# Blocked loads of q and k with VectorE transposes in place of TensorE transposes, for the last two batch pairs of a retention and FFN kernel

## The chip, the cores and the metric

The kernel runs on one core of a Trainium2 chip. The metric is the device time of one execution in microseconds. Three executions of the kernel before took 886.32, 886.95 and 888.02 us; the median is 886.95 us. A further execution was recorded by the hardware profiler, and every figure of the profile is from that one.

## The reference

Two blocks follow each other, all in float32 (weights arrive as float64):

```python
# retention: q, k, v are (8, 8, 576, 64) = batch, heads, sequence, head_dim
scores = matmul(q, k.T) / sqrt(64)
gamma  = 1 - 2 ** (-5 - arange(8))            # one per head
Dmat   = where(i >= j, gamma ** (i - j), 0)   # i, j: positions
attn   = matmul(scores * Dmat, v)
# bridge: (B, H, S, D) -> (B*S, H*D) = (4608, 512)
a = x @ w1; b = x @ w2                        # d_model 512, d_ff 1024
out = ((a * b) @ w3) @ w_out
```

The kernel writes the decay as a product: q is multiplied by gamma^i / sqrt(64) and v by gamma^-j, with a triangular mask in each chunk and a running state over the chunks before it. Both decay tables are inputs of the launch (`decay_q` of 8 x 576, `decay_k` of 576 x 8).

## The kernel before

**Chunks.** Batches are taken in four pairs. The sequence of 576 is cut into NC = 5 chunks, the first of 64 tokens and four of 128. A chunk g (0 to 19) is chunk g mod 5 of pair g div 5; it holds 2 batches x 8 heads. Chunks 5, 10 and 15 are the short ones.

**One chunk.** `load` (line 100) brings q, k and v with tokens in the 128 partitions, each as one DMA of 256 B runs (one head's 64 floats). `scale` (162) multiplies q or v by its decay on GpSimd. `front` (174) turns k and q: for each batch and pair of heads one TensorE transpose (line 185) of tokens x 128 features, 8 for k and 8 for q, into four PSUM tiles, which ScalarE copies to `kT` and `qT` (188). `score` (191) multiplies them (200) and VectorE masks the result into `pm` (203). `state` (207) adds k^T v of the chunk to a running PSUM tile (221), except in the last chunk of a pair, and copies it (225); it reads k with tokens in the partitions. `pv` (228) forms the output: state times qT (249, not in a pair's first chunk) and pm times v (256).

**FFN.** `up` computes one quarter of the hidden width for 2 x 192 tokens as seven TensorE products (451); VectorE sums them (456) and multiplies the two halves (477) as its last operation. Before the first quarter of a token block `strassen_tokens` (425) forms sums of the tokens, on GpSimd in the part of interest. `down` multiplies 2 x 128 tokens by the merged last weights (557), with VectorE sums (561), and issues its stores (602) on SP's queue. `carry` (509) is one ScalarE copy.

**Order.** The schedule is written by hand: each engine runs its instructions in the order in which the code emits them. SP's queue, too, issues DMAs in emitted order and waits for a buffer before a load. The first pair (chunks 0 to 4) runs among the conversion of weights. Then a loop over steps g = 5 to 19 emits, in each step, the load of q and k of chunk g+2, the scaling of v and the `front` of chunk g+1, about half of the step's work items, `pv(g)`, the load of v of g+2, `state` and `score` of g+1, the scaling of q of g+2, and the rest of the work items. A work item is an `up`, a `down` or a `carry`; they come from a list that a finished pair refills. From step 10 on a step has three or four of them, before that one. The two that stand ahead of `pv` are, for instance, two `up` in steps 10, 12, 14 and 17, an `up` and then a `down` in 11, 15 and 18, a `down` and then an `up` in 13, an `up` and a `carry` in 16.

**Buffers.** The tiles of loaded q, k and v have two buffers each, `kT` one in this loop, `qT` two, `pm` one, the output tile of `down` one. PSUM has seven rotating accumulation tiles (`acc`) and one for the state.

Of the kernel before, what the change touches and what calls it, by code (L numbers as in the profile page):

```python
# [8 lines left out]
F32 = mybir.dt.float32  # L9
I32 = mybir.dt.int32  # L10
U32 = mybir.dt.uint32
ALU = mybir.AluOpType
PSUM = bass.MemoryType.PSUM

# [19 lines left out]
def kernel(  # L36
# [13 lines left out]
    nc = tc.nc  # L50
    moe_w1, moe_w2, moe_w3, moe_w_out = (
        w.bitcast(I32).rearrange("r (c t) -> r c t", t=2) for w in (moe_w1, moe_w2, moe_w3, moe_w_out))
    B, H, S, D = q.shape
# [3 lines left out]
    P = 128  # L57
    NP = H // 2
# [3 lines left out]
    NC = (S + P - 1) // P  # L62
    short = S - (NC - 1) * P
    sizes = [short] + [P] * (NC - 1)
    starts = [0] + [short + c * P for c in range(NC - 1)]
    G = NB2 * NC
# [9 lines left out]
    const = ctx.enter_context(tc.tile_pool(name="const", bufs=1))  # L76
# [8 lines left out]
    pools = {}  # L85

    def open_attention(part):
        for nm in ("ld", "fr"):
            pools[nm] = part.enter_context(
                tc.tile_pool(name=nm, bufs=2, side="right", reuse_waits="tile"))  # L90

    open_attention(att_part)
    acc = ctx.enter_context(tc.tile_pool(name="acc", bufs=7, space=PSUM))
    st_ps = ctx.enter_context(tc.tile_pool(name="st_ps", bufs=1, space=PSUM))

    ctx.enter_context(tc.manual_schedule())

    live = {}

    def load(g, names, engine=nc.sync):  # L100
        i, c = divmod(g, NC)
        sz = sizes[c]
        src = {"k": k, "q": q, "v": v}
        for nm in names:
            t = pools["ld"].tile([P, 2 * H, D], F32, tag="ld_" + nm, name="ld_" + nm)
            engine.dma_start(
                t[:sz], src[nm][2 * i:2 * i + 2, :, starts[c]:starts[c] + sz, :].rearrange("b h p d -> p (b h) d"))
            live[nm, g] = t
# [13 lines left out]
    nc.vector.memset(lim[:, 1:2], 255.0 * 2.0 ** 23)  # L122
    gk = const.tile([P, NC, H], F32, tag="gk", name="gk")
    gq = const.tile([P, NC, H], F32, tag="gq", name="gq")
    dq = ffn.tile([P, 4, 2, TB], F32, tag="c", name="dq", bufs=1).rearrange("p a b s -> p (a b s)")[:H, :S]
    nc.scalar.dma_start(dq, decay_q)
    nc.scalar.dma_start(gk[:short, 0, :], decay_k[:short, :])
# [4 lines left out]
    for c in (0, slice(1, NC)):  # L132
        n = short if c == 0 else P
# [8 lines left out]
    def A(fp, nm):  # L142

        h, m = divmod(fp, 2)
        if nm in ("S1", "S2", "S4"):
            return wS[h][:, ("S1", "S2", "S4").index(nm), m]
        r, f = {"A11": (0, 0), "A12": (1, 0), "A21": (0, 1), "S3": (0, 1), "A22": (1, 1)}[nm]
        return wA[h][:, :, 2 * r:2 * r + 2, m * QC + f * P:m * QC + f * P + P]

    def strassen_weights(fp):  # L150
        def tt(out, in0, in1, op):
            nc.vector.tensor_tensor(out=A(fp, out), in0=A(fp, in0), in1=A(fp, in1), op=op)

        tt("S1", "A21", "A22", ALU.add)
        tt("S2", "S1", "A11", ALU.subtract)
        yield
        tt("S3", "A11", "A21", ALU.subtract)
        tt("S4", "A12", "S2", ALU.subtract)
        live["S", fp] = True
        yield  # L160

    def scale(g, nm, scalar=False):
        c = g % NC
        sz = sizes[c]
        t, gam = live[nm, g], {"q": gq, "v": gk}[nm]
        t = t[:sz].rearrange("p (b h) d -> p b h d", b=2)
        if scalar:
            for h in range(H):
                nc.scalar.mul(t[:, :, h, :], t[:, :, h, :], gam[:sz, c, h:h + 1])
            return  # L170
        nc.gpsimd.tensor_tensor(  # L171
            out=t, in0=t, in1=gam[:sz, c].unsqueeze(1).unsqueeze(3).to_broadcast([sz, 2, H, D]), op=ALU.mult)

    def front(g, names="kq"):
        c = g % NC
        sz = sizes[c]
        for nm in names:
            src = live[nm, g]
            dst = pools["fr"].tile([P, 2, NP, P], F32, tag=nm + "T", name=nm + "T",
                                   bufs=1 if nm == "k" and g >= NC else 2)  # L180
            for b in range(2):
                tp = acc.tile([P, NP, P], F32, tag="acc", name="tp")
                for p in range(NP):
                    h = b * H + 2 * p
                    nc.tensor.transpose(tp[:, p, :sz],  # L185
                                        src[:sz, h:h + 2, :].rearrange("p a d -> p (a d)"),
                                        ident[:sz, :sz])
                nc.scalar.copy(dst[:, b, :, :sz], tp[:, :, :sz])
            live[nm + "T", g] = dst

    def score(g):
        c = g % NC
        sz = sizes[c]
        kT, qT = live["kT", g], live["qT", g]
        pm = pools["fr"].tile([P, 2, 2, NP, P], F32, tag="pm", name="pm", bufs=1)
        for b in range(2):
            sc = [acc.tile([P, NP, P], F32, tag="acc", name="sc") for j in range(2)]
            for p in range(NP):
                for j, hs in enumerate(heads):
                    nc.tensor.matmul(sc[j][:sz, p, :sz], kT[hs, b, p, :sz], qT[hs, b, p, :sz],  # L200
                                     start=True, stop=True)
            for j in range(2):
                nc.vector.tensor_mul(pm[:sz, b, j, :, :sz], sc[j][:sz, :, :sz],  # L203
                                     mask[:sz, :sz].unsqueeze(1).to_broadcast([sz, NP, sz]))
        live["pm", g] = pm

    def state(g):
        c = g % NC
        sz = sizes[c]
        if c == NC - 1:  # L210
            return
        kn, vs = live["k", g], live["v", g]
        if c == 0:
            live["st"] = st_ps.tile([P, 2, NP, D], F32, tag="st", name="st")
        st = live["st"]

        for b in range(2):
            for p in range(NP):
                for j, hs in enumerate(heads):
                    h = b * H + 2 * p + j  # L220
                    nc.tensor.matmul(st[hs, b, p, :], kn[:sz, h, :], vs[:sz, h, :],  # L221
                                     start=(c == 0 and b == 0 and p == 0), stop=(c == NC - 2),
                                     skip_group_check=True)
        sb = pools["fr"].tile([P, 2, NP, D], F32, tag="sb", name="sb")
        nc.scalar.copy(sb, st)
        live["sb", g + 1] = sb
# [309 lines left out]
    def ahead(x, y, n=3):  # L536
        todo_sums = pair_of(x, y)[2]
        for _ in range(min(n, len(todo_sums))):
            aside.append(todo_sums.pop(0))
# [75 lines left out]
    score(0)  # L615
    scale(0, "v")
    state(0)
    convert_up_to(1)
    pv(0)
# [8 lines left out]
    scale(1, "v")  # L628
    score(1)
    state(1)  # L630
    convert_up_to(3)
    load_block()
    convert_up_to(4)
    first_sums = strassen_weights(0)
    next(first_sums)
    pv(1)
# [12 lines left out]
    convert(2)  # L649
    score(2)  # L650
    state(2)
    scale(3, "v", True)
    front(3, "q")
# [18 lines left out]
    att_part.close()  # L672


    pools["ab3"] = weights_part.enter_context(tc.tile_pool(name="ab3", bufs=1, side="right", reuse_waits="tile"))
    pools["wst"] = w3_part.enter_context(tc.tile_pool(name="wst", bufs=2, side="right", reuse_waits="tile"))
    w3op = ctx.enter_context(tc.tile_pool(name="w3op", bufs=1, reuse_waits="tile"))
# [60 lines left out]
    def work(n):  # L738
        for _ in range(min(n, len(todo))):
            fn, *args = todo.pop(0)  # L740

            nxt = next((x for x in todo if x[0] is not carry), None)
            if nxt and nxt[0] is down and fn is not carry:
                if fn is down:
                    args.append(nxt[1:])
                else:
                    last = args == [*every[max(nxt[1][0], nxt[2][0])], NQ - 1]
                    ahead(*nxt[1:], 1 if last else 3)
            fn(*args)
# [4 lines left out]
    state(NC)  # L754
    score(NC)
    scale(NC + 1, "q")
    for g in range(NC, G):
        c = g % NC
        n = -(-len(todo) // (NC - c))
        if g + 2 < G:  # L760
            load(g + 2, "kq")
        if g + 1 < G:
            scale(g + 1, "v")
            front(g + 1)
        work((n + 1) // 2)
        pv(g)
        if g + 2 < G:
            load(g + 2, "v")
        if g + 1 < G:
            state(g + 1)  # L770
            score(g + 1)
        if g + 2 < G:
            scale(g + 2, "q")
        if g == NC + 1:
            strassen_tokens(1, 0)
            todo.extend((up, 1, 0, fp) for fp in range(2))
        work(n // 2)
        if c == NC - 1:
            add_pair(g // NC)
# [44 lines left out]
```

## Time and profile before

| | |
|---|---|
| median of three executions | 886.95 us (886.32 to 888.02) |
| the profiled execution | 887.59 us, its span 885.9 us, mean TensorE clock 0.998 |
| TensorE busy (PE) | 866.6 us, 98% |
| VectorE / ScalarE / GpSimd busy | 433.7 / 212.4 / 111.1 us |
| all PE transposes of q and k | 320, of which 160 belong to chunks 10 to 19 |
| GpSimd scaling of q (line 171) | 18 of 1.9 us |
| DMA moved | 59.73 MB, 110,592 of the packets being 256 B runs of q, k and v |

The span is what the profiler saw from the first to the last instruction; the execution's own time is a little more. In the profile PE is TensorE's matmul, PEld its weight load, DVE VectorE, ACT ScalarE, POOL GpSimd and SPq the queue of SP. L185 is line 185 of the kernel. A row of a timeline gives the start in us from the span's start, the time in us, engine, line, operation, `output<-input`, and in brackets how long the engine was idle before it and what ended that. The chain is followed back from the last instruction through whatever released each step; rows of it give start, time and what ran.

### The profile page before, as it was taken

Reading aid. Unit: us, or ns where it says so; the run is one execution under the profiler, and the core shown is the slowest. Engines: PE = TensorE matmul, PEld = TensorE weight load, DVE = VectorE, ACT = ScalarE, POOL = GpSimd, SP = SyncE. Lnnn points to the kernel's source line nnn. Section 1 sums busy time; section 2 is a strip of 40 time slices with the busy share of each in tenths; the row PEclk is TensorE's granted clock in tenths of the full one; section 3 lists DMA queues with packets and bytes.
Section 4 is the critical chain, followed back from the end, with each engine's and each line's share of the span. In section 5 each row is a group of like instructions: output and inputs, shape, how many; then the busy total and the mean of one; then the engine's idle time right before and its main releaser. Section 6 shows DMA issues by size and latency. Waiting matters only on the chain.

```text
span 885.9 us, 15255 instructions
## 1 busy us (share of the span) xinstructions
PE 866.6 (98%) x6517; PEld 792.8 (89%) x6517; DVE 433.7 (49%) x763; ACT 212.4 (24%) x426; POOL 111.1 (13%) x82
## 2 busy tenths in 40 slices
PE   5899999999999999999999999999999999999998
PEld 4799999544889999999999999999999999999997
DVE  3799998971543243433434433433433424434343
ACT  3676334552122212111121111211110111001000
POOL 3000020003003223002112121221200101000000
PEclk9999999999999999999999999999999999999999
DMA  9993332427046533134033134022100000000001
GB/s 184 217 229 99 96 118 97 143 95 107 0 108 124 105 60 73 26 72 96 1 72 61 25 72 95 1 57 40 26 24 24 1 24 1 24 24 1 24 1 47
DMA packets 125555, 59.73 MB, mean 67 GB/s; under 512 B 113704, under 2 KB 113704, under 8 KB 125488
## 3 DMA queue, kind: packets, MB, share of 16 engines
q1 hardware_dynamic: 123824, 58.47, 29.9%
q8 instruction: 51, 0.84, 0.4%
q10 hardware_dynamic: 1664, 0.30, 0.2%
q14 instruction: 16, 0.13, 0.1%
HBM read 49.32 MB, written 9.44 MB: 66 GB/s over the span
## 4 chain that ended last, share of the span: by engine, by line
PE 89%; DVE 3%; issue 1%; DMA 1%; ACT 1%; ACTq 0%; SPq 0%; DVEq 0%
PE up L451 45%; PE po L557 24%; PE ps L406 6%; PE xps L256 4%; PE sc L200 3%; PE tp L185 3%; PE xps L249 2%; PE st L221 1%; DVE c L456 1%; PE tp L396 1%; DVE e L341 0%; DMA raw<-in_moe_w_dram 0%; ACT e L330 0%; DVE w L350 0%; DVE ab L477 0%
## 5 line engine op out<-in xcount | busy, mean ns | idle before, releaser
L456 DVE TENSOR_TENSOR c<-up,c 128x384 f32<-128x384 f32 x240 | 133.6, 557 | 224.3 <-PE up L451 218.0
L451 PE MATMUL up<-xT,wA 128*128 128x192 f32 x1152 | 212.6, 328 | 0.9 <-ACT xT L261 0.9
L451 PEld LDWEIGHTS up<-xT,wA 128*128 128x128 f32 x1152 | 191.0, 191 | 3.2 <-ACT xT L261 1.1
L451 PE MATMUL up<-T,wS 128*128 128x192 f32 x768 | 141.7, 328 | 2.1 <-DVE T L425 2.1
L451 PEld LDWEIGHTS up<-T,wS 128*128 128x128 f32 x768 | 128.3, 191 | 2.4 <-issue 2.4
L557 PE MATMUL po<-w3o,ab 128*128 128x256 f32 x456 | 104.1, 380 | 0.3 <-ACT ot L579 0.3
L557 PEld LDWEIGHTS po<-w3o,ab 128*128 128x128 f32 x456 | 85.9, 190 | 12.2 <-ACT ot L579 0.7
L471 ACT COPY c<-up 128x384 f32<-128x384 f32 x48 | 22.9, 477 | 228.1 <-PE up L451 223.9
L561 DVE TENSOR_TENSOR ot<-po,ot 128x256 f32<-128x256 f32 x90 | 38.2, 424 | 74.8 <-PE po L557 74.2
L451 PE MATMUL up<-xT,wS 128*128 128x192 f32 x384 | 70.6, 327 | 0.6 <-DVE c L456 0.5
L451 PE MATMUL up<-T,wA 128*128 128x192 f32 x384 | 70.3, 326 | 0.0
L203 DVE TENSOR_TENSOR pm<-sc,mask 128x512 f32<-128x512 f32 (+1 forms) x80 | 45.5, 629 | 48.0 <-PE sc L200 48.0
L557 PE MATMUL po<-wB,forms 128*128 128x256 f32 x288 | 65.1, 379 | 0.0
L451 PEld LDWEIGHTS up<-xT,wS 128*128 128x128 f32 x384 | 63.6, 190 | 1.5 <-DVE c L456 1.5
L451 PEld LDWEIGHTS up<-T,wA 128*128 128x128 f32 x384 | 63.7, 190 | 0.0
L557 PEld LDWEIGHTS po<-wB,forms 128*128 128x128 f32 x288 | 54.7, 190 | 7.4
L171 POOL TENSOR_TENSOR ld_q<-ld_q,gq 128x1024 f32<-128x1024 f32 (+1 forms) x18 | 34.8, 1931 | 209.7 <-DMA ld_q<-in_q_dram 204.4
L406 PE MATMUL ps<-wo,w3T 128*128 128x512 f32 x128 | 56.4, 593 | 0.2 <-ACT w3T L398 0.2
L171 POOL TENSOR_TENSOR ld_v<-ld_v,gk 128x1024 f32<-128x1024 f32 (+1 forms) x17 | 32.3, 1900 | 176.5 <-DMA ld_v<-in_v_dram 144.1
L425 POOL TENSOR_TENSOR T<-xT,T 128x384 f32<-128x384 f32 x20 | 21.2, 1058 | 228.9 <-PE up L451 227.2
L477 DVE TENSOR_TENSOR ab<-c 128x768 f32<-128x768 f32 x48 | 46.4, 967 | 3.8
L406 PEld LDWEIGHTS ps<-wo,w3T 128*128 128x128 f32 x128 | 23.7, 190 | 27.3 <-issue 26.8
(72 smaller groups left out, 829.1 us busy)
## 6 DMA issues: line engine op xcount, KB each, us to landing
raw<-in_moe_w_dram SPq DMA_DIRECT2D x24, 512.0 KB, 3.8
ld_k<-in_k_dram SPq DMA_DIRECT2D x16, 512.0 KB, 6.5
ld_q<-in_q_dram SPq DMA_DIRECT2D x16, 512.0 KB, 7.1
ld_v<-in_v_dram SPq DMA_DIRECT2D x16, 512.0 KB, 4.7
out_dram<-ot SPq DMA_DIRECT2D x24, 256.0 KB, 2.1
raw<-in_moe_w_dram SPq DMA_DIRECT2D x16, 256.0 KB, 6.4
raw<-in_moe_w_out_dram SPq DMA_DIRECT2D x8, 512.0 KB, 3.5
out_dram<-ot SPq DMA_DIRECT2D x24, 128.0 KB, 2.4
```

The source lines that it names most:

```text
L171: nc.gpsimd.tensor_tensor(out=t, in0=t, in1=gam[:sz, c].unsqueeze(1).unsqueeze(3).to_broadcast([sz, 2, H, D]), op=ALU.mult)
L185: nc.tensor.transpose(tp[:, p, :sz], src[:sz, h:h + 2, :].rearrange("p a d -> p (a d)"), ident[:sz, :sz])
L200: nc.tensor.matmul(sc[j][:sz, p, :sz], kT[hs, b, p, :sz], qT[hs, b, p, :sz], start=True, stop=True)
L203: nc.vector.tensor_mul(pm[:sz, b, j, :, :sz], sc[j][:sz, :, :sz], mask[:sz, :sz].unsqueeze(1).to_broadcast([sz, NP, sz]))
L256: nc.tensor.matmul(banks[r][heads[half], b, n, :sz], vs[:sz, b * H + 2 * p + j, :], pm[:sz, b, j, p, :sz], start=(c == 0 and m == 0), stop ...
L406: nc.tensor.matmul(ps, live["w3T", ft][:, g, :], live["wo"][:, g, :], start=(g == 0), stop=(g == KF - 1))
L451: nc.tensor.matmul(ps[:, w, :], a[:, w, r, :], b[:, r, :], start=(new and w == r == 0), stop=(w == r == 1), skip_group_check=True)
L456: nc.vector.tensor_add(c[:, to], ps, c[:, sb])
L471: nc.scalar.copy(c[:, 0], p1)
L477: nc.vector.tensor_mul(ab[:, 4 * fp:4 * fp + 4, :], c[:, :, 0, :], c[:, :, 1, :])
L557: nc.tensor.matmul(ps[nm], a[A][:, f, :], live["W"][B][:, f, :], start=(f == 0 and not on), stop=(f == NP - 1), skip_group_check=True)
L561: nc.vector.tensor_add(ot[:, to[0], to[1]], ps[nm], ot[:, sb[0], sb[1]])
```

## The change

For chunks 10 to 19 the TensorE transposes are replaced. q and k are loaded a second way, `load_blocks`: each 32 tokens x 32 features block of a head goes to the partitions where its features will stand once transposed, with the 32 tokens in those 32 partitions and the features along the free dimension. A chunk of 128 tokens needs 4 feature groups x 4 token groups = 16 DMAs for q and 16 for k, each of 32 partitions, 8 segments and 128 B runs; a chunk of 64 tokens needs half as many. Then one VectorE transpose (32x32 blocks) for k and one for q writes the whole of `kT` and `qT`. The scaling of q, two GpSimd operations of 512 elements per partition, is done on the blocks, with decays in a new constant tile `gqs`, filled by 16 small DMAs with 4 B runs. k is still loaded the plain way, too, for `state`, except in the last chunk of a pair. The blocked tiles use the two buffers of the plain q tile.

In the loop, for such chunks: the loads of k and blocks of g+2 are emitted after `pv(g)` and the load of v, not at the step's start; the scaling of q of g+1 comes after the first work item, and the transposes of g+1 after the second, directly ahead of `pv(g)`. In step 9, which has one work item, both come after it. The sequence of the work items is as before.

```diff
+    gqs = const.tile([P, NP, S // 32], F32, tag="gqs", name="gqs")
...
+    BL = 32
+    def load_blocks(g, nm):
+        i, c = divmod(g, NC)
+        n = sizes[c] // BL
+        t = pools["ld"].tile([P, 2 * NP, P // BL, BL], F32, tag="ld_q", name="bl_" + nm)
+        src = {"k": k, "q": q}[nm][2 * i:2 * i + 2].rearrange("b (p a) s d -> a (b p) s d", a=2)
+        for a in range(2):
+            for f in range(D // BL):
+                part = (a * (D // BL) + f) * BL
+                for m in range(n):
+                    s0 = starts[c] + m * BL
+                    nc.sync.dma_start(t[part:part + BL, :, m, :],
+                                      src[a, :, s0:s0 + BL, f * BL:(f + 1) * BL].rearrange("m r x -> r m x"))
+        live["bl_" + nm, g] = t
+    def scale_blocks(g):
...
+        for b in range(2):
+            part = t[:, b * NP:(b + 1) * NP, :n, :]
+            nc.gpsimd.tensor_tensor(
+                out=part, in0=part, in1=gqs[:, :, n0:n0 + n].unsqueeze(3).to_broadcast([P, NP, n, BL]),
+                op=ALU.mult)
+    def front_blocks(g):
...
+        for nm in "kq":
+            dst = pools["fr"].tile([P, 2, NP, P], F32, tag=nm + "T", name=nm + "T", bufs=1 if nm == "k" else 2)
+            nc.vector.transpose(
+                dst[:, :, :, :sizes[c]].rearrange("p b m (n x) -> p (b m) n x", x=BL),
+                live["bl_" + nm, g][:, :, :n, :])
+            live[nm + "T", g] = dst
...
     att_part.close()
+    for a in range(2):
+        for f in range(D // BL):
+            part = (a * (D // BL) + f) * BL
+            for p in range(NP):
+                nc.sync.dma_start(gqs[part:part + BL, p, :], decay_q[2 * p + a].rearrange("(n r) -> r n", r=BL))
...
+    in_blocks = [u >= 2 * NC for u in range(G)] + [False] * 2
     for g in range(NC, G):
         c = g % NC
         n = -(-len(todo) // (NC - c))
-        if g + 2 < G:
+        if g + 2 < G and not in_blocks[g + 2]:
             load(g + 2, "kq")
         if g + 1 < G:
             scale(g + 1, "v")
-            front(g + 1)
-        work((n + 1) // 2)
+            if not in_blocks[g + 1]:
+                front(g + 1)
+        half = (n + 1) // 2
+        if in_blocks[g + 1]:
+            work(1)
+            scale_blocks(g + 1)
+            work(1)
+            front_blocks(g + 1)
+            half = max(half - 2, 0)
+        work(half)
         pv(g)
         if g + 2 < G:
             load(g + 2, "v")
+        if in_blocks[g + 2]:
+            if (g + 2) % NC != NC - 1:
+                load(g + 2, "k")
+            load_blocks(g + 2, "k")
+            load_blocks(g + 2, "q")
         if g + 1 < G:
             state(g + 1)
             score(g + 1)
-        if g + 2 < G:
+        if g + 2 < G and not in_blocks[g + 2]:
             scale(g + 2, "q")
```

More of the change, by code (lines that the diff above doesn't have):

```diff
@@ L160, in strassen_weights @@
         yield
+    BL = 32
[13 more added lines that the diff above has]
+    def scale_blocks(g):
+        c = g % NC
+        n, n0 = sizes[c] // BL, starts[c] // BL
+        t = live["bl_q", g]
+        for b in range(2):
[4 more added lines that the diff above has]
+    def front_blocks(g):
+        c = g % NC
+        n = sizes[c] // BL
+        for nm in "kq":
[4 more added lines that the diff above has]
+            live[nm + "T", g] = dst
     def scale(g, nm, scalar=False):
@@ L211, in state @@
             return
-        kn, vs = live["k", g], live["v", g]
+        vs = live["v", g]
+        kn = live["k", g]
         if c == 0:
```

## The prediction

> **What bounds the kernel now.** I read the page's busy times first, then the chain that ended last, then VectorE and the DMA queue's issues around one step.
>
> The page, busy time and chain by engine:
>
> ```profile
> PE 866.6 (98%) x6517; PEld 792.8 (89%) x6517; DVE 433.7 (49%) x763; ACT 212.4 (24%) x426; POOL 111.1 (13%) x82
> PE 89%; DVE 3%; issue 1%; DMA 1%; ACT 1%; ACTq 0%; SPq 0%; DVEq 0%
> ```
>
> TensorE is the bound. Whatever leaves it shortens the run, and whatever makes it wait lengthens it. The chain in order of time (start, us, what), three stretches; a step g is named by its pv:
>
> ```profile
> 331.52 1.03 PE xps L249 x32
> 332.55 1.90 PE xps L256 x32
> 334.45 1.02 PE st L221 x30
> ...
> 336.45 1.90 PE tp L185 x16
> ...
> 356.56 1.08 PE xps L256 x32
> 357.63 1.08 PE st L221 x32
> 358.72 1.99 PE sc L200 x32
> ...
> 567.25 9.10 PE up L451 x56
> 576.35 1.03 PE xps L249 x32
> 577.38 1.90 PE xps L256 x32
> 579.28 0.93 PE st L221 x32
> 580.21 1.99 PE sc L200 x32
> ```
>
> The first is pv of step 9 with the PE transposes of chunk 11 behind it, the second pv of step 10 (a first chunk of 64 tokens, so no L249), the third step 16. From a pv's start to the score behind it PE has 3.86 us of other work in step 16 and only 2.16 us in step 10. VectorE there (timeline, same columns):
>
> ```profile
> 576.38 0.56 DVE L456 TENSOR_TENSOR c<-up,c 128x384 f32<-128x384 f32 x1 [2.04 <-PE up L451]
> 577.05 0.96 DVE L477 TENSOR_TENSOR ab<-c 128x768 f32<-128x768 f32 x1
> ```
>
> After an `up`, VectorE is done 1.66 us into pv (578.01 - 576.35); after a `down` 0.46 us into it (last L561, 405.06 + 0.42 against 405.02). The issues on SP's queue and on ACT's, from their timelines:
>
> ```profile
> 473.54 2.25 SPq L106 DMA_DIRECT2D ld_q<-in_q_dram  x1
> 505.82 0.37 SPq L106 DMA_DIRECT2D ld_v<-in_v_dram  x1
> 64.89 1.25 SPq L291 DMA_DIRECT2D raw<-in_moe_w_dram  x2
> 1.58 0.79 ACTq L126 DMA_DIRECT2D dq<-decay_q_dram  x1
> ```
>
> An issue over 128 partitions takes 0.37 us with a free queue; two over 64 partitions take 1.25 us, 0.65 us apart with the gap; one over 8 partitions 0.79 us. A full load right behind another takes 2.0 to 2.3 us[...].
>
> [...] The trace has no VectorE transpose. Its two-source rows (384 elements 557 ns, 768 elements 967 ns) give 1.07 ns per element and 0.15 us fixed. [...] Here 256 B runs move at 221 to 240 GB/s in 410 to 416 us, 18.6 ns per run on each of 16 engines. [...]
>
> **What is removed.** The 16 PE transposes of each of chunks 10 to 19, from the chain: 0.98, 1.90, 1.75, 1.75, 1.90, 1.14, 1.75, 1.75, 1.75, 1.75 = **16.4 us**, all on the path. With them go four ACT copies of 0.6 us a chunk (ACT is 24% busy) and two accumulation tiles; both were hidden and are worth nothing. POOL's scaling of q (1.90 us) goes too.
>
> **What is added.** (1) *gqs*: 16 DMAs behind the raw loads of the early weight phase. At 0.65 us that is 10.4 us of SP. The raw load issued at 116.0 goes into the buffer freed by the block five before it, and its own block is read first near 136; 16 us are left after a 4 us landing, so it costs nothing. Its 9,216 runs of 4 B take at most 10.7 us of the 16 engines at 18.6 ns each, under the same cover. If that cover were gone, the one delay of 10 us would count. (2) *Block loads*: 32 issues a step (16 for 64-token chunks) behind v and, except for last chunks, k. In runs, 8192 of 128 B: 4.8 us at half of 18.6 ns, 9.5 us at the full value; either is under the issue time. The old q load, and k at the step's start, go. (3) *Scalings*: two POOL operations of 512 elements, 1.2 us each between the rows of 384 (1.06) and 1024 (1.90): 2.4 us. (4) *Two VectorE transposes* of 1024 elements. [...] 1.25 us each, 2.6 us with hand-overs, near 1.4 for a short chunk.
>
> **VectorE's order.** The transposes stand behind the second work item's sums and ahead of the mask products of the score; they end 1.66 + 2.6 = 4.26 us into pv after an `up`, 3.06 after a `down`. The score of chunk g+1 needs both. Stall against the start of that score in the trace: steps 9 and 14 (short chunk next) none; 10: 4.26 - 2.16 = 2.1; 11: none; 12, 16, 17: 0.4 each; 13: 4.26 - 2.93 = 1.3; 15: 3.06 - 2.16 = 0.9; 18: 0.1. Sum 5.6 us. Behind the waiting transposes nothing but those mask products queues.
>
> **SP's order.** v waits for the end of pv(g), as before; then k, then the blocks. For a full chunk: pv 2.9, v 0.5, k 2.1[...] = 5.5 us after pv's start; 32 issues; 2.0 us landing of the last (the stores' row: 2.0 to 3.5); 2.4 us scaling; 1.3 us transposing q. What does an issue over 32 partitions cost? Between 0.40 with gap (the 128-partition row) and 0.85 (the 8-partition row); I take the 64-partition pair, 0.65. Then q is ready 5.5 + 20.8 + 2.0 + 2.4 + 1.3 = 32.0 us after pv's start. Time to the score that needs it, PE transposes taken out:
>
> - loaded in step 9, used in 10: 358.72 - 331.52 - 1.90 = 25.3 us: stall 6.7, in place of the 2.1;
> - loaded in 8, used in 9 (16 issues): ready 4.7 + 10.4 + 2.0 + 1.3 + 0.8 = 19.2 against 335.47 - 316.32 - 0.98 = 18.2: stall 1.0;
> - loaded in 12 without k: 3.5 + 26.5 = 30.0 against 30.0: within VectorE's 1.3;
> - loaded in 10, 11, 14, 15, 16, 17: 50, 37, 41, 35, 49 and 51 us: covered.
>
> Stores of a `down` behind block loads start up to some 10 us late; each next `down` comes at least an `up` (9.1 us) later, so output tiles stay covered. Waits of the added operations on many loads: an estimate of 0.15 us a step, 1 us, from the 17 to 51 ns of the wait instructions shown.
>
> **Sum.** Loss 5.6 - 2.1 + 6.7 + 1.0 + 1.0 = 12.2; gain 16.4; net 4.2 us faster. The profiled execution took 887.59 us (span 885.9, 1.7 around it), so 883.4 there; against the median 886.95, 0.6 above which the profiled one lies, **882.7**.
>
> **Rivals.**
> - *Almost all the gain arrives.* At 0.45 us an issue[...], steps 9 and 10 aren't late for loads: loss 5.6 + 1 = 6.6, time 877[...]. For: 128-partition issues take 0.37. Against: everything narrower took 0.5 to 0.8.
> - *SP's issues become the bound (slower).* Place: 32 small issues between a pv and the score of the next step. Each 0.01 us more costs 0.16 us in step 9, 0.32 in step 10 and, past 0.69, 0.32 in step 13. Loss equals gain at 0.72 us an issue; at 0.85 it is 4.2 + 13.1 + 1.2 + 6.4 + 2.9 in steps 9, 10, 12, 13, 16, 1.4 in the others, 1.0 waits: 30, so 900. For: issue time grew from 128 to 64 partitions. Against: the 0.79 is a first issue on another queue.
> - *Transposes at half rate (slower).* They take 4.6 us a pair and end 6.3 us into pv, 5.1 after a `down`: 4.2 to 1.2 us in each full step, 7.9 in step 10 with its loads: 27.7 in all, time 898. It turns slower when a pair takes about 3.1 us. [...]
> - *No effect*: only if the freed PE time were already idle. The chain has PE on it throughout, so this is small beyond a chance meeting of gain and loss.
>
> **Chances.** Forecast and near it (878 to 887) 0.43; most of the gain (below 878) 0.17; SP as bound 0.23; slow transposes 0.15; no effect 0.02. This kernel's measurement can tell about 0.2%, 1.8 us. Of the first case a fifth lies within that: faster 0.52, same 0.10, slower 0.38. The likeliest case's own range is 878 to 887. Eight in ten reaches from part of the better case to both slow ones: 874 to 900.
>
> **What would show it.** No PE transposes after 336 us; two VectorE transposes a chunk of about 1.25 us; 32 issues about 0.65 us apart on SP after each pv; a PE wait ahead of the score of about 7 us in step 10, 1 to 2 in steps 13 and 15, none in step 11. If transposes take 2 us, or issues 0.8, the sign turns. A PE wait inside the early weight phase would mean that gqs was not covered.

## The result and the profile after

Four executions of the changed kernel took 879.61 to 882.07 us, median **881.54 us**, against 887.12 us for the kernel before beside them: a ratio of 0.9933, 95% interval 0.9915 to 0.9951. It is 5.6 us faster; 4.2 were forecast. The profiled execution was the quickest of the four (879.61 us, span 877.6).

From the page, busy time and the chain by engine:

```profile
PE 851.1 (97%) x6357; PEld 777.6 (89%) x6357; DVE 458.7 (52%) x783; ACT 193.7 (22%) x386; POOL 112.2 (13%) x92
PE 85%; DVE 5%; SPq 2%; issue 2%; DMA 0%; ACT 0%; DVEq 0%; POOL 0%; POOLq 0%; ACTq 0%
```

TensorE has 160 instructions and 15.5 us less; VectorE has 25 us more, of which 22.4 are transposes. VectorE and SP's queue now have a share in the chain: the gain has a bill. What VectorE and SP pay for one item, from the views of the two blocked tiles (duration in ns: least, median, most; then the start of the first and the last in us):

```profile
L179 SPq DMA_DIRECT2D bl_k<-in_k_dram x144: 311/449/3447, 319.1 to 628.5; - x144
L198 DVE STREAM_TRANSPOSE kT<-bl_k x10: 705/1236/1239, 330.5 to 665.7; 128x1024 f32<-128x1024 f32 x8, 128x512 f32<-128x512 f32 x2
```

An issue takes 0.45 us and a transpose of 1024 float32 elements 1.24 us. Step 10, in the timelines of SP, GpSimd, VectorE and TensorE:

```profile
332.33 1.43 SPq L109 DMA_DIRECT2D ld_k<-in_k_dram  x1
333.86 11.15 SPq L179 DMA_DIRECT2D bl_k<-in_k_dram  x16
345.12 7.82 SPq L179 DMA_DIRECT2D bl_q<-in_q_dram  x16
...
354.82 2.06 POOL L189 TENSOR_TENSOR bl_q<-bl_q,gqs 128x512 f32<-128x512 f32 x2 [16.49 <-DMA bl_q<-in_q_dram]
...
356.91 1.25 DVE L198 STREAM_TRANSPOSE qT<-bl_q 128x1024 f32<-128x1024 f32 x1 [1.87 <-POOL bl_q L189]
...
358.30 3.78 PE L241 MATMUL sc<-qT,kT 64*128 64x128 f32 x32 [3.92 <-DVE qT L198]
```

This is the chain of step 10, read upwards from the score: TensorE waited 3.92 us for `qT`, VectorE for GpSimd's scaling, GpSimd for blocks of q that SP issued last at 352.9. The first sixteen issues took 11.15 us, the next sixteen 7.82. And the score itself took 3.78 us instead of 1.99. The view by stretches of time says why (last three columns: granted clock, DMA share, GB/s):

```profile
354.00:356.00 2.00, 0.38 (x14) 0.24 (x10) 1.04 (x1) 0.59 (x1) 1.18 (x2) 1.00 0.77 176
356.00:358.00 2.00, 0.00 (x0) 0.00 (x0) 1.09 (x1) 0.00 (x0) 1.92 (x3) 0.81 1.05 211
358.00:360.00 2.00, 1.70 (x16) 1.73 (x18) 0.15 (x1) 0.00 (x0) 2.00 (x3) 0.50 1.16 197
360.00:362.00 2.00, 2.00 (x20) 1.79 (x18) 1.29 (x2) 0.00 (x0) 2.00 (x2) 0.50 0.34 48
362.00:364.00 2.00, 2.00 (x8) 1.99 (x7) 1.29 (x2) 0.00 (x0) 0.68 (x1) 0.50 0.37 58
```

With TensorE idle from 354.4, the granted clock fell to half for 6.8 us. Score and the `up` behind it took 3.78 + 10.29 us where they took 1.99 + 9.30 before: 2.8 us on top of the wait. Wait and slower work together are the loss of this step.

Step 12 is the common case (VectorE and TensorE):

```profile
439.69 0.96 DVE L519 TENSOR_TENSOR ab<-c 128x768 f32<-128x768 f32 x1
440.57 1.24 DVE L198 STREAM_TRANSPOSE kT<-bl_k 128x1024 f32<-128x1024 f32 x1
441.73 1.20 DVE L198 STREAM_TRANSPOSE qT<-bl_q 128x1024 f32<-128x1024 f32 x1
...
443.08 2.06 PE L241 MATMUL sc<-qT,kT 64*128 64x128 f32 x32 [0.22 <-DVE qT L198]
```

The transposes follow the last product of the `up` without a gap and end just after TensorE is ready for the score: a wait of 0.22 us.

**Loss by step.** To compare kernels with the same TensorE order, I take the time from one pv's start to the next pv's start and subtract that of the kernel before without the PE transposes in it. Step 12, for example: 27.52 - (28.94 - 1.90) = 0.5. In the last row but one, the forecast is the 1.0 us for the added wait instructions, and the measured columns are the interval from pv(8) to pv(9). In us:

| step | forecast | changed | k last | twice | own place | between |
|---|---|---|---|---|---|---|
| 9 | 1.0 | 0.2 | 0.2 | 1.3 | 7.4 | 0.8 |
| 10 | 6.7 | 6.7 | 2.4 | 6.4 | 0.0 | 0.0 |
| 11 | 0 | 0.0 | 0.0 | 1.6 | 0.0 | 0.0 |
| 12 | 0.4 | 0.5 | 0.5 | 4.7 | 0.2 | 0.2 |
| 13 | 1.3 | 1.0 | 1.0 | 5.2 | -0.2 | -0.2 |
| 14 | 0 | 0.0 | 0.0 | 0.7 | 0.0 | 0.0 |
| 15 | 0.9 | 0.7 | 0.7 | 4.8 | 0.0 | 0.0 |
| 16, 17, 18 | 0.9 | 0.6 | 0.6 | 12.8 | 0.0 | 0.3 |
| 8 and waits | 1.0 | 0.0 | 0.0 | 0.0 | 0.0 | 0.7 |
| sum | 12.2 | 9.7 | 5.4 | 37.4 | 7.4 | 1.8 |

The changed loop thus gained 16.4 - 9.7 = 6.7 us in its profile. The rest of that profile's 8.3 us of span was there at 48 us, before the first added instruction: the PE transposes ahead of pv(2) began at 48.27 instead of 49.90 us. It isn't the work of the change. From 34.5 to 37.9 us TensorE was busy throughout in both profiles, but at a granted clock of 0.50 before and of 1.00 after, and half of 3.4 us is 1.7. This first part varies from profile to profile: pv(3), up to which all versions run the same instructions, began between 66.2 and 68.5 us in the eight profiles of this document. The interval from there to the `up` ahead of pv(8) is 257.30 us after and 257.32 before, so the 16 small loads of `gqs`, which lie in it, cost nothing:

```profile
101.36 11.17 SPq L721 DMA_DIRECT2D gqs<-decay_q_dram  x16
```

### The profile page after: what moved, and what is told of

It reads as the page before. It is cut to its first block, busy times and chain, and to the rows that moved or that the text cites. A ratio compares the mean times of both kernels' runs of the same rounds, so it can differ in the third digit from the quotient of the medians.

```text
span 877.6 us, 15316 instructions
## 1 busy us (share of the span) xinstructions
PE 851.1 (97%) x6357; PEld 777.6 (89%) x6357; DVE 458.7 (52%) x783; ACT 193.7 (22%) x386; POOL 112.2 (13%) x92
## 4 chain that ended last, share of the span: by engine, by line
PE 85%; DVE 5%; SPq 2%; issue 2%; DMA 0%; ACT 0%; DVEq 0%; POOL 0%; POOLq 0%; ACTq 0%
PE up L493 44%; PE po L599 24%; PE ps L448 6%; PE sc L241 4%; PE xps L298 3%; SPq L179 2%; PE tp L226 1%; PE xps L291 1%; DVE c L498 1%; PE st L263 1%; DVE qT L198 1%; PE tp L438 1%; DVE kT L198 1%; DVE e L383 0%; DMA bl_q<-in_q_dram 0%
## 5 line engine op out<-in xcount | busy, mean ns | idle before, releaser
L599 PEld LDWEIGHTS po<-w3o,ab 128*128 128x128 f32 x456 | 85.9, 190 | 12.2 <-ACT ot L621 0.6
L513 ACT COPY c<-up 128x384 f32<-128x384 f32 x48 | 22.9, 478 | 226.4 <-PE up L493 222.2
L506 ACT COPY c<-up 128x384 f32<-128x384 f32 x48 | 22.9, 477 | 132.7 <-PE up L493 84.0
L448 PEld LDWEIGHTS ps<-wo,w3T 128*128 128x128 f32 x128 | 23.7, 190 | 27.3 <-issue 26.8
L241 PE MATMUL sc<-qT,kT 64*128 64x128 f32 (+1 forms) x640 | 40.6, 280 | 6.4 <-DVE qT L198 6.4
```

The costliest lines, as they stand in the source:

```text
L448: nc.tensor.matmul(ps, live["w3T", ft][:, g, :], live["wo"][:, g, :], start=(g == 0), stop=(g == KF - 1))
L506: nc.scalar.copy(c[:, 0], p1)
L513: nc.scalar.copy(c[:, 0], p1)
L599: nc.tensor.matmul(ps[nm], a[A][:, f, :], live["W"][B][:, f, :], start=(f == 0 and not on), stop=(f == NP - 1), skip_group_check=True)
```

## The experiments

All change the changed kernel and keep TensorE's order, unless said otherwise. The theory (A in each) is that the gain is the removed PE transposes and the losses are lateness ahead of the score: SP's issues in step 10, VectorE's order in the others.

### One DMA moved: k last

```diff
-            if (g + 2) % NC != NC - 1:
-                load(g + 2, "k")
             load_blocks(g + 2, "k")
             load_blocks(g + 2, "q")
+            if (g + 2) % NC != NC - 1:
+                load(g + 2, "k")
```

> The changed kernel with one move on SP's queue: the plain load of k of chunk g+2 is issued behind the 32 block loads instead of ahead of them. TensorE, VectorE and GpSimd run the same instructions in the same order. Theory A (in step 10 SP's issues are late, because the first block loads wait behind v and k[...]): the block loads of chunk 11 end about 4.8 us earlier (1.45 for k's issue, 3.3 for the stretched first sixteen, 11.15 us in place of 7.8), TensorE's wait in step 10 falls from 3.9 us to VectorE's floor of about 2.1, and the stretch of half granted clock behind it (6.8 us, about 2.8 us lost) goes: about 877, 4.6 us less than the changed kernel. Theory B (landing or the scaling on GpSimd sets it, not the issue): the wait stays at 3.5 to 4 us and the time at 881 to 882.

878.16 us (877.64 to 879.06), ratio to the kernel before 0.9902 (0.9886 to 0.9919), 3.4 us less than the changed kernel's median. SP and TensorE in step 10:

```profile
334.45 10.00 SPq L179 DMA_DIRECT2D bl_k<-in_k_dram  x16
344.57 7.78 SPq L179 DMA_DIRECT2D bl_q<-in_q_dram  x16
...
357.21 1.15 PE L263 MATMUL st<-ld_v,ld_k 128*64 128x64 f32 x32 [1.84 <-DMA ld_k<-in_k_dram]
358.75 2.06 PE L241 MATMUL sc<-qT,kT 64*128 64x128 f32 x32 [0.38 <-DVE qT L198]
```

The issues of the blocks end 18.4 us after v's issue instead of 21.0, 2.6 us earlier and not 4.8, because k's own 1.43 us went but the first sixteen, now right behind v, still took 10.00 us. That was enough: the loss of step 10 is 2.4 us, near VectorE's floor, the score runs at full clock, and nothing else changed (table). Now the plain k arrives just as late, and `state` waits for it: 1.84 of the 2.2 us. VectorE would have held the score as long. Theory A stands in its mechanism, with 3.4 us gained in place of 4.6: TensorE's waits fell by 1.7 us (from 3.92 to 2.22), and step 10 lost 4.3 us less, because the half-speed stretch went with them.

### Twice as many issues

```diff
-                    nc.sync.dma_start(t[part:part + BL, :, m, :], ...)
+                    for b in range(2):
+                        hp = slice(b * NP, (b + 1) * NP)
+                        nc.sync.dma_start(t[part:part + BL, hp, m, :], ...)
```

> The changed kernel with each block load cut in two (one per batch): 64 issues a full step instead of 32, the same bytes and the same 128 B runs. Theory A (the count of issues sets how late blocks are, 0.49 us each): a full step's blocks end 16 to 18 us later; against the room seen in the changed kernel that is a wait of about 19 us in step 10, 13 in 13, 9 in 12, 8 in 16, 5 in 15 and 7 in 9: about 940. Theory B (the movement of 128 B runs on the DMA engines sets it): nothing changes, 880 to 884.

939.18 us (two executions, 937.51 and 940.86), ratio 1.0587 (1.0559 to 1.0614). Same bytes and same runs, 57.6 us more: it is the count of issues, not the movement of 128 B runs. The slower rival of the prediction exists, at twice the count. SP, ScalarE and TensorE between pv(14) and pv(15):

```profile
537.81 18.19 SPq L181 DMA_DIRECT2D bl_k<-in_k_dram  x32
556.10 15.27 SPq L181 DMA_DIRECT2D bl_q<-in_q_dram  x32
...
575.21 0.37 ACT L623 COPY ot<-po 128x256 f32<-128x256 f32 x1 [17.18 <-DMA out_dram<-ot]
...
575.63 3.78 PE L601 MATMUL po<-w3o,carry 128*128 128x256 f32 x8 [13.37 <-ACT ot L623]
```

Reckoned as in the table, the losses were 8.8 us in step 9, 16.1 in 10, 10.2 in 12, 5.3 in 13, 15.6 between pv(14) and pv(15), 0.7 in 15, 9.1 in 16 and 1.4 in 17. That the total came within 1 us of the 940 expected was luck: steps 13 and 15 lost 6.0 us where 18 were expected, and 15.6 us were lost where none were, as I had left out the output tile. The `down` behind pv(14) can't store until SP has issued 64 blocks, so the next `down` waits for that tile (the lines above). With 32 issues SP issues those stores from 524.16 us on, the last one of which the trace tells the landing has landed at 527.83, and the next `down` writes the tile at 528.24, when its product is there and not later. That cover is the one the prediction named, and it is 0.4 us thick there.

### Each transpose twice

```diff
-            nc.vector.transpose(dst..., live["bl_" + nm, g]...)
+            for again in range(2):
+                nc.vector.transpose(dst..., live["bl_" + nm, g]...)
```

> The changed kernel with each VectorE transpose done twice into the same place. Theory A (the score waits for VectorE in order, so a transpose ahead of pv is on TensorE's path once it ends after pv and state): 1.2 us more in step 10, about 1.7 in 11, 2.45 each in 12, 13, 15, 16, 17 and 18, about 1.2 in 9 and 0.6 in 14: 19 us more, about 900; up to 3 us more wherever [...]the granted clock falls as it did in step 10. Theory B (VectorE's transposes are hidden, and the measured losses are hand-overs): about 882 to 885.

908.81 us (907.31 to 909.71), ratio 1.0243 (1.0227 to 1.0259): 27.3 us more, where 19 had been worked out from VectorE's order and up to 3 for each fall of the clock. The longest and the shortest of seven of TensorE's waits ahead of the score:

```profile
360.49 2.89 PE L242 MATMUL sc<-qT,kT 64*128 64x128 f32 x23 [4.49 <-DVE qT L199]
...
694.82 3.18 PE L242 MATMUL sc<-qT,kT 64*128 64x128 f32 x32 [2.42 <-DVE qT L199]
```

The waits in steps 10, 12, 13, 15, 16, 17 and 18 are 4.49, 2.78, 3.71, 3.19, 2.79, 2.78 and 2.42 us; those in the other steps are at most 1.49. With each of the seven the record of the granted clock has a half-speed stretch, 6.8 us with the first and 3.4 with each other, so also with waits well under the 3.92 us of the changed kernel's step 10. The six steps from 12 on lost 24.6 us more than in the changed kernel, where VectorE's order gave 14.7; half of six stretches of 3.4 us is 10.2, which is about the difference. Step 10 lost 0.3 us less, not 1.2 more: its wait is longer, but 2.9 us of its half-speed stretch pass while TensorE waits, against 1.1 in the changed kernel. VectorE's order is thus the cause of the small losses, and a transpose pair of 5 us instead of 2.5 would have made the change a loss, as the second slower rival said.

### The old place

The blocks, but load, scaling and transposes where the kernel before has them:

```diff
         if g + 1 < G:
             scale(g + 1, "v")
-            if not in_blocks[g + 1]: front(g + 1)
+            front_blocks(g + 1) if in_blocks[g + 1] else front(g + 1)
+        if in_blocks[g + 2]:
+            ...load k of g + 2 unless last; load_blocks k, q of g + 2
+        work((n + 1) // 2)
...
+            scale_blocks(g + 2) if in_blocks[g + 2] else scale(g + 2, "q")
```

> The two parts of the change taken apart: blocks and VectorE transposes are kept, but load, scaling and transposes stand where the kernel before has its load of q and k, its scaling of q and its front: transposes of chunk g+1 at the start of step g, block loads of g+2 right behind them, scaling of g+2 behind the score. TensorE's order is unchanged. Theory A (losses come from the place directly ahead of pv): the transposes are hidden behind the work items, the losses of steps 11 to 18 (2.8 us) go, and only step 10 may be late, because the blocks of chunk 11 are issued at the start of step 9, 14 us ahead of their use, which they miss by about 5 us with VectorE's later sums behind them: 874 to 880. Theory B (VectorE's 2.4 us a step cost TensorE wherever they stand): 881 to 884.

878.41 us (877.79 to 879.16), ratio 0.9902 (0.9887 to 0.9917). VectorE and TensorE ahead of pv(10), in the code the start of step 10, in the table row 9:

```profile
344.18 1.25 DVE L198 STREAM_TRANSPOSE qT<-bl_q 128x1024 f32<-128x1024 f32 x1 [7.57 <-POOL bl_q L189]
...
347.25 2.93 PE L493 MATMUL up<-xT,wS 128*128 128x192 f32 x8 [4.77 <-DVE c L498]
```

Steps 11 to 18 lose nothing now: VectorE's 2.4 us a step are free behind a work item. But the blocks of chunk 11 are again late for their transposes, VectorE stands 7.57 us in front of the sums of the `up`, and TensorE waits for those: 4.77 us and half a clock for 6.8 us, 7.4 together. In the changed kernel the same blocks cost 6.9 us (rows 9 and 10), so the later place had saved 0.5 us with them and cost 2.8 us in the other steps.

### Between the work items

```diff
+            scale_blocks(g + 1)
+            if half > 1:
+                work(1)
+                half -= 1
+            front_blocks(g + 1)
+        if in_blocks[g + 2]:
+            ...load k of g + 2 unless last; load_blocks k, q of g + 2
         work(half)
         pv(g)
```

> The changed kernel with its additions moved, TensorE's order as it was: VectorE's transposes of chunk g+1 stand between the two work items ahead of pv (in step 9, with one item, ahead of it), the block loads of g+2 right behind them, and the scaling on GpSimd at the step's start. Theory A (all 9.7 us of loss in the changed kernel are lateness ahead of the score, from SP's issues in step 10 and VectorE's order elsewhere): no TensorE wait for kT or qT is left, the half-clock stretch behind step 10 is gone, and the whole 16.4 us of the removed transposes arrive: 870 to 872. Theory B (transposes on VectorE or the many small loads cost TensorE something wherever they stand): 874 or more.

874.12 us (871.41 to 874.21), ratio 0.9837 (0.9822 to 0.9852): the best of all, 13.4 us under the kernel before beside it, though not the 870 to 872 expected; by its number alone it falls to theory B (874 or more). The table tells them apart: the losses are not spread over the steps, as B would have it. Steps 8 and 9 lose 1.5 of the 1.8 us, because q's scaling is late for VectorE there, now by 3.7 and 0.8 us, and an `up` waits for its sums. The scaling stands on GpSimd behind that of v, whose load had landed only just before (at 324.6 and 346.5 us). Of the waits for `qT` one of 0.22 us is left, in step 16, and there is no half-speed stretch in the loop. The loop itself, pv(8) to pv(19), takes 375.22 us against 389.79: 14.6 us less. Of the other 1.2 us, 0.7 lie ahead of pv(3), which began at 68.53 us in this profile and at 67.81 in that of the kernel before; that is the variation of the first part described above. The rest is less than the spread of the executions. Transposes, loads and scaling were moved together here; what each move gave alone is told only by the two versions before.

### Sixteen idle PE transposes put back

The version just described, with TensorE turning a constant tile sixteen times per chunk, its result unread. The place is not quite the old one: where two work items stand ahead of pv, the idle transposes come between them (chunk 12's at 391.13 us, behind the `up`) and not ahead of both, as in the kernel before (382.08):

```diff
             front_blocks(g + 1)
+            for r in range(4):
+                tp = acc.tile([P, NP, P], F32, tag="acc", name="tp")
+                for p in range(NP):
+                    nc.tensor.transpose(tp[:, p, :n1], mask[:n1, :], ident[:n1, :n1])
```

> The version before this one, with sixteen TensorE transposes per chunk put back for chunks 10 to 19 at the old place; they turn a constant tile and nothing reads their result, so blocks, scaling and VectorE's transposes still feed the score. It adds only the removed TensorE work. Theory A (each removed transpose lay on TensorE's path): 16.4 us more than without them, 886 to 888, level with the kernel before. Theory B (part of that time was cover for other waits): less than 12 us more.

888.51 us (886.39 to 889.37), ratio to the kernel before 1.0006 (0.9997 to 1.0014): level with it, 14.4 us above the version without. In each of the intervals pv(10) to pv(18) the kernel before is met within 0.04 us. So the removed work lay on the path in full, and the blocks, the scaling and VectorE's transposes, all still there, cost nothing beside it. The 2 us short of 16.4 are the losses of steps 8 and 9 and of the small waits, which the restored work hides again: pv(8) to pv(19) takes 389.90 us.

## Why the prediction was right

- **The sum.** The losses came out at 9.7 us where 12.2 had been summed: 1.0 less for the waits of the added operations, 0.8 less in step 9, 0.7 less from VectorE. The loop gained 6.7 us in the profile, the medians differ by 5.6, and 4.2 were forecast.
- **The gain.** 16.4 us of PE transposes, all on the path: shown by the restored transposes.
- **gqs, ScalarE's copies, PSUM at nothing.** gqs: 257.30 against 257.32 us over its stretch. It was issued at 101 us, not behind the load at 116 that I had named, and took 0.70 us apiece. ScalarE and PSUM appear in no new wait of TensorE; they weren't tried alone.
- **VectorE's order.** 1.24 and 1.20 us against 1.25, and step for step the losses of the table, 2.8 us for steps 11 to 18 against 3.5. The 1.25 was my estimate; no trace then showed a VectorE transpose, but the two-source rows' 1.07 ns per element and 0.15 us fixed give 1.25 us for 1024 elements too. The trace after has 1.24 us for 1024 and 0.71 for 512 float32 elements, that is 1.04 ns each and 0.17 us fixed. The half-rate rival reckoned with twice 1.07 ns per element, 4.6 us a pair; a pair took 2.44, so it is out.
- **Waits of the added operations.** 1.0 us forecast, none found: in step 12, behind an `up`, the first transpose starts at 440.57 us, when the multiplication of the halves (0.96 us from 439.69 on) is just ending, and the second follows without a gap.
- **SP's order.** The mechanism was right, and the size of step 10 came out right for a wrong reason. An issue over 32 partitions cost 0.49 us with its gap, not the 0.65 of 64-partition ones. On the other side the first sixteen issues, right behind the loads of v and k, took 11.15 us, a delay that I had charged to k only. q was ready 29.3 us after pv(9) began (358.16 - 328.89), not 32.0, and TensorE waited 3.9 us, not 6.7. The clock's 2.8 us, which I had left out of every term, filled the gap: that the step's loss is the forecast one is luck. With the forecast wait of 6.7 us and a falling clock the step would have cost more than the sum held.
- **Stores covered.** Held at 32 issues, ahead of pv(15) by no more than 0.4 us; shown by its failing at 64.
- **The slower rival on SP.** Its break-even of 0.72 us per issue was built without the clock; the run with 64 issues confirms its sign and its steps (9, 10, 12, 13 and 16), not that number. One of the two largest losses of that run, the 15.6 us at the output tile, is at a place that the rival did not have.

## What to carry to other kernels

Take work off the bounding engine for its full time, then find for each substitute the last wait in front of the bound: here the places of two VectorE transposes, the scaling and the block loads made the difference between 5.6 and 13.4 us, and twice the number of DMA issues made a loss of 52 us. Put a substitute between two long items of the bounding engine, not directly ahead of its consumer, and start its loads right behind the step that frees their buffers. When you price a wait of TensorE as long as those that came with a half-speed stretch here (2.42 us and more), add what the clock lost with them, here 1.7 to 2.8 us.

## What the runs showed that I had not expected

Waits of TensorE of 2.42 us and more in front of the score each came with 3.4 us, or a multiple of it, at half the granted clock; waits of 1.84, 1.49 and 1.15 us did not. The length of a wait alone doesn't settle its price: 3.92 us in the changed kernel brought 6.8 us at half speed, and 3.94 us in step 13 of the version with 64 issues brought 3.4.

The traces say what does. In the version with each transpose twice the half-speed stretches of steps 10 to 18 begin 27, 9, 22, 11, 15 and 15 times 3.413 us apart; the stretch in the trace of the kernel before (at 34.5 us) is 3.413 us long, that of step 10 of the changed kernel 6.827, twice as much. In these traces the clock thus changed on a fixed grid of 3.413 us. Two windows of that grid with the window behind each (length, TensorE's busy time and count, the other engines', granted clock, DMA share, GB/s), in steps 12 and 11:

```profile
446.34:449.76 3.42, 1.27 (x22) 1.30 (x24) 2.07 (x3) 0.95 (x2) 0.00 (x0) 1.00 1.03 188
449.76:453.17 3.41, 3.41 (x20) 2.81 (x18) 2.47 (x4) 0.00 (x0) 1.90 (x1) 0.50 0.40 62
...
408.80:412.21 3.41, 2.00 (x52) 1.86 (x48) 3.38 (x3) 1.66 (x3) 0.00 (x0) 1.00 0.40 99
412.21:415.62 3.41, 3.33 (x40) 3.21 (x41) 2.16 (x5) 0.00 (x0) 1.34 (x1) 1.00 1.25 228
```

With TensorE busy for 1.27 us of a window the next one ran at half speed, with 2.00 us it did not. In the seven traces that have a half-speed stretch to fix the grid by, and between 150 and 860 us, all 15 full-speed windows with up to 1.8 us of busy TensorE are followed by a half-speed one, and none with 2.0 us or more is. So a window in which TensorE had been busy for half of the time, 1.8 of 3.4 us (step 10 of the version with each transpose twice), was still followed by half speed. In these runs a wait therefore cost in steps, by how it fell on the windows: 3.9 us became 6.7, and 2.2 us, spread over two windows, stayed 2.4.

Issue time on SP does not follow the number of partitions in one direction: 0.33 to 0.39 us for 128 behind a pause of SP's queue, 0.47 to 0.67 for 64, 0.31 to 0.34 for block loads over 32 and 0.45 within their row, and 0.50 for the loads of `gqs` in their row, over 32 too. The runs of these DMAs differ as well, and no version varied the partitions alone.
